# An attention kernel's last reciprocals, branch, closing products, first keys and order of work

## The chip, the cores and the metric

The kernel runs on one core of one Trainium2 chip. A core has five engines that run side by side, each with a list of instructions in a fixed order: PE (matmuls; its weight loads are shown apart as PEld), DVE (VectorE), ACT (ScalarE), POOL (GpSimd) and SP (SyncE), which here issues DMAs. Engines wait for one another through semaphores. The metric is the time of one execution on the device, in microseconds (us); lower is better. A profile gives the start and length of each instruction of one execution.

## The reference

Two attention layers read two inputs of 2048 x 512; their outputs stand side by side. Cut to what matters:

```python
# A: 32 query heads of 16, one shared key and value head
q = (x @ wq).reshape(B, S, 32, 16);  k = x @ wk;  v = x @ wv
p = softmax(einsum("bhqd,bkd->bhqk", q, k) * 16**-0.5)
a = einsum("bhqk,bkd->bhqd", p, v).reshape(B, S, 512) @ wo
# B: linear attention, 32 heads of 16
phi(t) = concat(softmax(t @ w_phi), softmax(-(t @ w_phi)))
o = phi(q) @ (phi(k).T @ v) / (phi(q) @ phi(k).sum(0) + 1e-6)
b = o.reshape(B, S, 512) @ wo
out = concat(a, b)
```

A's exponentials are nearly all of the work: 32 heads x 2048 queries x 2048 keys.

## The kernel before, in words

**Tiles of A.** Scores are made keys down, queries across. A unit is 128 keys x 512 queries of one head: one matmul with 32 rows of contraction (L1672). Four heads make a quad and use the four row groups of PE. A stage `sc` of 0 to 31 is eight heads' even or odd half for 512 queries: 16 quads, one per 128 keys (`kap`). Most quads go to ACT, which takes the exponential of three units (1536 columns) and of two units (1024 columns) by turns, out of PSUM banks 0 to 2 and 3 to 4 (L1733; jobs `qk` for the scores and `ex` for the exponential). While ACT reads one group of banks, PE may fill the other only. The other quads (`dq`) are done on DVE: it turns scores into the bits of an exponential with a multiply and an add (L1834, `dz`), adds shifts to make three further terms (two on DVE, L1852, `dS`; one on POOL, L1849, `dP`), and PE sums the four terms (L1889, `dpv`). The products with the values (L1778, `pv`; L1889) gather in one PSUM bank, `ACC`. The values carry a block of ones, so that 16 rows of each 32 in `ACC` are sums of exponentials, the denominators, and 16 are numerators; even and odd stages have them the other way round.

**End of a stage.** DVE copies `ACC` to SBUF (`ac`, L1449). SP's DMAs gather the denominators (L1905), DVE takes reciprocals (`rc`, L1913), four DMAs put them back as one row per group of 32 (L1918), and four more spread each row over 16 partitions (L1924). POOL, in the last stages DVE, multiplies (`on`, L1931). For odd stages DMAs then move the rows (L1937). PE multiplies by `wo` (L1950; for the last 512 queries, in parts, `pp`, L1970).

**The last stage (31)** goes another way, in `finish_last`, in two halves of 256 queries. DVE copies the denominators over each group of 32 partitions out of `ACC` (stream shuffle, L1980), ACT takes a logarithm (L1982) and an exponential of its negative (L1983), which is the reciprocal, DVE multiplies (L1996), and PE adds the last part of the output product (L2004) to parts made before (L1970). ACT and DVE copy the four results out (L2014, L1449), and four DMAs of 128 KB write them (L2016).

**Start.** POOL fills a tile with ones and one with zeros; PE multiplies them ten times (`WARM`, L1443). Then it makes the first queries and the first 512 keys by turns (L1604), 512 columns each. ACT copies the queries (L1610), DVE the keys with the even half masked out and with the odd half masked out (L1616). A first score group needs the queries and the masked keys.

**Other work** between: all of B, spread over the run by release times; zero products (L1443 and L1426) where the plan leaves PE idle.

**What sets the order.** `_Fast.run` places jobs one by one on a modelled time line with fixed durations, by earliest start and rank; `SEEDS` holds a number for each 20 us of modelled time, which shakes the ranks and picks among a few settings. The result is one fixed list per engine. The chip runs each list in that order, and only semaphores set the times.

**The branch.** Whether the inputs stay in the bounds that this fast path needs is computed as a flag. Each engine reads it and branches; DVE and SP do so before their last pieces (`cut`), so that their last instructions stand behind a jump. In `plan`, DVE's cut is set from its last nine jobs.

## Time and profile before

| | us |
|---|---|
| median of 3 runs (740.68 to 740.93) | 740.73 |
| the profiled execution | 740.4 |
| its span | 738.7 |
| ACT busy | 719.0 (97%) |
| PE busy | 696.7 (94%) |
| DVE busy | 676.7 (92%) |
| POOL busy | 316.8 (43%) |
| granted PE clock, mean | 0.994 of full speed |

The span runs from the profile's first to its last record; the execution's time has 1.7 us more around it. "Busy" counts an instruction from its start to its end; instructions of ACT and of PE overlap their neighbours a little, so a mean duration is longer than the pitch from one start to the next. In a timeline row stand start, length, engine, line, operation, output<-input, sizes, a count where several are merged, and in brackets the idle time before it and what ended it.

### The profile page before, as it was taken

To read this page: it belongs to the slowest core of one execution; us is meant where nothing else is said; L and a number is where in the kernel's file an instruction comes from. 1 tells how busy PE (TensorE), PEld (TensorE's weight loads), DVE (VectorE), ACT (ScalarE), POOL (GpSimd) and SP (SyncE) were. 2 spreads that over 40 slices of the span, in tenths; PEclk is the share of its full clock that TensorE was granted. 3 is DMA by queue.
4 is the path that set the end of the run, shared out by engine and by line. 5 is a ranking of instruction groups with operands and counts; after the bars stand their busy time and mean duration, and the time that the engine had idled before them with its cause. 6 is when DMAs were issued, how large, how long until landed. Compare 5 with 4: busy or idle time off the path is not lost.

```text
span 738.7 us, 17787 instructions
## 1 busy us (share of the span) xinstructions
PE 696.7 (94%) x7467; PEld 227.5 (31%) x7467; DVE 676.7 (92%) x1134; ACT 719.0 (97%) x675; POOL 316.8 (43%) x248
## 2 busy tenths in 40 slices
PE   8999999999999999999999999999999999999995
PEld 3233233323332222223332322233333333333331
DVE  4999999999999999997999999899999999999992
ACT  6999999999999999999999999999999999999993
POOL 6335453542535435447343534444443443334441
PEclk9999999999999999999999999999999999999997
DMA  9820011110111101111011111011111111112102
GB/s 191 190 32 6 8 8 10 12 9 6 10 12 17 30 7 8 13 9 9 7 8 19 23 23 12 3 19 17 30 20 8 15 22 27 23 18 25 16 20 40
DMA packets 47552, 18.13 MB, mean 25 GB/s; under 512 B 38500, under 2 KB 45604, under 8 KB 47464
## 3 DMA queue, kind: packets, MB, share of 16 engines
q1 hardware_dynamic: 45736, 16.62, 17.2%
q8 instruction: 60, 0.98, 0.5%
q10 hardware_dynamic: 1728, 0.30, 0.2%
q14 instruction: 28, 0.23, 0.1%
HBM read 2.15 MB, written 4.19 MB: 9 GB/s over the span
## 4 chain that ended last, share of the span: by engine, by line
ACT 85%; PE 9%; DVE 3%; DMA 1%; POOL 1%; SPq 1%; issue 0%; POOLq 0%; DVEq 0%
ACT f_PT L1733 81%; PE f_ps L1672 3%; ACT f_Ek L2121 2%; ACT f_ET L2214 2%; PE f_ps L1889 1%; DVE f_Z L1834 1%; PE f_ps L1778 1%; PE f_ps L1443 1%; DVE f_Z L1852 1%; PE f_ps L2300 1%; POOL f_Z L1849 1%; PE f_ps L1662 1%; DMA f_denS<-f_denS 0%; PE f_ps L1970 0%; DMA f_denS<-f_denC 0%
## 5 line engine op out<-in xcount | busy, mean ns | idle before, releaser
L1733 ACT ACTIVATE f_PT<-f_ps 128x1536 bf16<-128x1536 f32 (+1 forms) x603 | 691.7, 1369 | 1.3 <-PE f_ps L1672 1.0
L1849 POOL TENSOR_TENSOR f_Z<-f_Z,f_step 128x1024 int32<-128x1024 int32 x135 | 255.3, 1891 | 352.8 <-DVE f_Z L1852 351.0
L1834 DVE TENSOR_SCALAR f_Z<-f_ps 128x512 int16<-128x512 f32 x540 | 351.5, 681 | 21.1 <-PE f_ps L1672 14.2
L1672 PE MATMUL f_ps<-f_QA,f_KR 32*128 32x512 bf16 x2048 | 303.9, 384 | 29.8 <-ACT f_PT L1733 16.8
L1852 DVE TENSOR_SCALAR f_Z<-f_Z 128x2048 int16<-128x2048 int16 x270 | 182.5, 694 | 1.5 <-PE f_ps L1889 0.4
L1672 PEld LDWEIGHTS f_ps<-f_QA,f_KR 32*128 32x128 bf16 x2048 | 78.9, 91 | 264.1 <-ACT f_PT L1733 167.5
L1889 PE MATMUL f_ps<-f_Z,f_VK 128*32 128x512 f16 x2160 | 141.1, 382 | 0.2
L1778 PE MATMUL f_ps<-f_PT,f_VA 128*32 128x512 bf16 x1508 | 124.3, 385 | 0.0
L1443 PE MATMUL f_ps<-f_ones,f_zero 128*128 128x512 bf16 (+8 forms) x281 | 65.8, 355 | 1.3 <-POOL f_zero L1469 1.3
L1889 PEld LDWEIGHTS f_ps<-f_Z,f_VK 128*32 128x32 bf16 x2160 | 45.5, 96 | 63.3 <-issue 26.4
L1778 PEld LDWEIGHTS f_ps<-f_PT,f_VA 128*32 128x32 bf16 x1508 | 26.7, 94 | 57.2 <-issue 55.3
L1443 PEld LDWEIGHTS f_ps<-f_ones,f_zero 128*128 128x128 bf16 (+2 forms) x281 | 18.7, 97 | 29.7 <-issue 23.7
L1426 PE MATMUL f_ps<-f_ones,f_zero 32*128 32x512 bf16 x74 | 26.1, 380 | 0.0
L1931 POOL TENSOR_TENSOR f_Od<-f_accS,f_denS 128x512 bf16<-128x512 f32 x14 | 17.8, 1269 | 16.1 <-DVE f_Z L1852 15.2
L2270 DVE TENSOR_TENSOR f_Wk<-f_ps,f_wq 128x512 bf16<-128x512 f32 x32 | 21.9, 683 | 0.6 <-PE f_ps L2260 0.4
L1449 DVE COPY f_accS<-f_ps 128x512 f32<-128x512 f32 x31 | 21.2, 683 | 1.4 <-PE f_ps L1778 0.9
L1931 POOL TENSOR_TENSOR f_On<-f_accS,f_denS 128x512 bf16<-128x512 f32 x14 | 17.8, 1271 | 9.8 <-DVE f_Z L1852 8.1
L2152 DVE TENSOR_TENSOR f_vS<-f_ps,f_rs 128x1024 bf16<-128x1024 f32 x16 | 19.4, 1217 | 1.5 <-PE f_ps L2142 1.5
L2127 DVE TENSOR_REDUCE f_ssum<-f_Ek 128x64 f32<-128x1024 bf16 x16 | 19.3, 1209 | 1.6 <-ACT f_Ek L2121 1.3
L2214 ACT ACTIVATE f_ET<-f_ps 128x512 bf16<-128x512 f32 x32 | 19.6, 744 | 0.0
L2121 ACT ACTIVATE f_Ek<-f_ps 128x512 bf16<-128x512 f32 x32 | 19.6, 756 | 0.0
L2300 PE MATMUL f_ps<-f_Bwo,f_oT 128*128 128x512 bf16 x64 | 16.6, 381 | 0.3 <-ACT f_ET L2214 0.3
(104 smaller groups left out, 339.4 us busy)
## 6 DMA issues: line engine op xcount, KB each, us to landing
f_denS<-f_denS SPq DMA_DIRECT2D x124, 30.0 KB, 3.1
out_dram<-f_outB SPq DMA_DIRECT2D x17, 128.0 KB, 2.0
f_denC<-f_accS SPq DMA_DIRECT2D x124, 2.0 KB, 1.7
f_denS<-f_denC SPq DMA_DIRECT2D x124, 2.0 KB, 1.7
out_dram<-f_outA SPq DMA_DIRECT2D x14, 128.0 KB, 2.2
f_On<-f_Od SPq DMA_DIRECT2D x60, 16.0 KB, 1.8
f_Bwv<-in_B_wqkv_dram SPq DMA_DIRECT2D x1, 512.0 KB, 4.3
f_Bwo<-in_B_wo_dram SPq DMA_DIRECT2D x1, 512.0 KB, 5.3
```

Source lines behind the costliest of these rows:

```text
L1426: self.add("pe", lambda pe: pe.matmul(out, lhsT=zero[0:32, :], rhs=rhs, start=False, stop=False, tile_position=(0, 0)), reads=["ones", "ze ...
L1443: mm = pe.matmul(ps[x:x + m, bank, 0:n].rearrange("p (a n) -> p a n", n=128), lhsT=zero[0:r, 0:m], rhs=rhs, start=start, stop=start, **kw)
L1672: return pe.matmul(self.ps[:, bank, :], lhsT=self.KR[32 * g:32 * g + 32, sc % 2, kap * 128:(kap + 1) * 128], rhs=self.QA[32 * g:32 * g + 3 ...
L1733: self.add("act", lambda a: a.activation(out=PT[:, sl[0]:sl[0] + size, :], in_=ps[:, b0:b0 + size, :], func=ACT.Exp), reads=[("PS", b0 + i ...
L1778: mm = pe.matmul(ps[32 * g:32 * g + 32, bank, :], lhsT=w, rhs=PT[:, slots[g], :], start=start, stop=stop, tile_position=(0, 32 * g))
L1834: self.add("dve", lambda v: v.tensor_scalar(out=o, in0=ps[:, bank, :], scalar1=self.Z1, scalar2=self.Z0, op0=ALU.mult, op1=ALU.add), reads ...
L1849: self.add("pool", lambda g: g.tensor_tensor(out=w(t), in0=w(0), in1=self.step3.to_broadcast([128, 256 * (b - a)]), op=ALU.add), reads=zk ...
L1852: self.add(eng, lambda v: v.tensor_scalar(out=Z[:, t, a:b], in0=Z[:, 0, a:b], scalar1=256.0 * t, scalar2=None, op0=ALU.add), reads=zk, wri ...
L1889: mm = pe.matmul(ps[32 * g:32 * g + 32, bank, :], lhsT=w[:, k, :], rhs=Zf[:, k, sl[g], :], start=start and k == 0, stop=stop and k == 3, t ...
L1931: self.add("pool" if sc < self.ONP else "dve", lambda v: v.tensor_tensor(out=o, in0=accS[:, r, :], in1=R[:, r, :], op=ALU.mult), reads=[(" ...
L2121: self.add("act", (lambda a, sg: (lambda e: e.activation(out=Ek[:, r, a].rearrange("p h f -> p (h f)"), in_=ps[:, bank, :], func=ACT.Exp, ...
L2214: self.add("act", lambda e: e.activation(out=self.ET[:, sl, :], in_=self.ps[:, bank, :], func=ACT.Exp, scale=sg), reads=[("PS", bank)], wr ...
```

## The change

Six edits:

1. For stage 30, the last with reciprocals by DMA, the four spreading DMAs are left out. A DVE stream shuffle over 128 x 512 (job `sh`) spreads the row; the multiplication `on` 30 waits for it.
2. DVE's cut: the last nine DVE jobs are sorted by planned start, the planned end of PE is appended, and the largest gap is always taken (before: only gaps over 0.5 us that begin over 5 us ahead of PE's end).
3. In the closing chain zero products may be put ahead of the last products where the plan has over two of them to spare, and the planned readiness of the two halves is a little later.
4. At the start PE makes the queries and the first 128 keys only, by turns; the whole first 512 keys follow as a projection of their own. DVE masks the 128 keys first (even half), then the other 384. The first score groups wait for the 128 alone.
5. Nine zero products at the start in place of ten; planned arrivals of the first input tile at 5.6 and 6.35 us (4.8 and 6.0 before).
6. New `SEEDS`, hence another order throughout. Each kind of work keeps its count, but for zero products and the pieces named above.

```diff
-    WARM = 10
+    WARM = 9
...
-            self.tw["AxT", 0, c] = ((4.8, 6.0, 6.0, 6.0)[c], "sp")
+            self.tw["AxT", 0, c] = ((5.6, 6.35, 6.35, 6.35)[c], "sp")
...
-                job(("pk", 0), "pe", 0.44, self.proj_first, mode="full", nb=2, prio=0)
+                job(("pf",), "pe", 0.54, self.proj_first, mode="full", nb=1, prio=0)
+                job(("qa", 0), "act", 0.478, self.proj_first2, after=[("pf",)], frees=[("pq", 0)], prio=0)
+                job(("KR0",), "dve", 0.25, lambda: self.proj_k3(0, 0, 128), after=[("pf",)], prio=0)
+                job(("pk", 0), "pe", 0.87, lambda: self.proj_k(0), after=[("pf",)], mode="full", nb=1, prio=0)
+                job(("KR", 0, 0), "dve", 0.52, lambda: self.proj_k3(0, 128, 512), after=[("pk", 0), ("KR0",)], prio=u)
...
+        job("sh", "dve", 0.85, self.spread, after=[("rc", 30)], prio=1.3)
...
-                after=[("rc", sc)] + ([("op", 4 * ((sc - 12) // 8) + i) for i in range(4)] if sc >= 12 else []))
+                after=[("rc", sc) if sc < 30 else "sh"] + ([("op", 4 * ((sc - 12) // 8) + i) for i in range(4)] if sc >= 12 else []))
...
-            for w, name, rd in ((self.wq[:, :, 0:128], ("pq", 0), ("wq", 0)), (self.wk_rep, ("pk", 0), "wk_rep")):
+            for w, name, rd, n in ((self.wq[:, :, 0:128], ("pq", 0), ("wq", 0), 512), (self.wk_rep, None, "wk_rep", 128)):
...
+    def kr(self, u):
+        return ("KR0",) if u[0] % 2 == 0 and u[1] == 0 else ("KR", u[0] % 2, u[1] // 4)
...
         self.dmas(fs, [("denR", r)], [("row", r), ("denS", r)], 1.8)
+        if sc == 30:
+            return
...
+    def spread(self):
+        R = self.denS[:, 0, :]
+        self.add("dve", lambda v: v.stream_shuffle(out=R, in_=R, mask=[0] * 16 + list(range(16, 32))), reads=[("row", 0), ("denS", 0)], writes=[("row", 0), ("denS", 0)])
...
-        ready = [t + 2.1, t + 2.8]
+        ready = [t + 2.15, t + 2.95]
...
+            k = int((ready[n] - t) / 0.2155) - 1
+            if k > 0:
+                self.fill(cols=(512,) * k, start=True, bank=next(b for b in self.free if b not in (6, 7)))
...
-    SEEDS = (841236, 504472, 983516, 719862, 658977, 503735, 772408, 265022, 493407, 762606, 12760, 907041, 734584,
+    SEEDS = (332850, 31012, 1022942, 986432, 402629, 324809, 0, 27406, 912665, 397942, 417505, 51469, 741216,
...
-        ends = [x for x in self.log if x[2] == "dve"][-9:]
-        gaps = [(b[0] - a[0] - a[1], n) for n, (a, b) in enumerate(zip(ends, ends[1:])) if a[0] + a[1] < self.te["pe"] - 5.0]
-        self.cut["dve"] -= 8 - max(gaps)[1] if gaps and max(gaps)[0] > 0.5 else 0
+        ends = sorted((x for x in self.log if x[2] == "dve"), key=lambda x: x[0])[-9:] + [(self.te["pe"], 0.0)]
+        gaps = [(b[0] - a[0] - a[1], n) for n, (a, b) in enumerate(zip(ends, ends[1:]))]
+        self.cut["dve"] -= 8 - max(gaps)[1]
```

With the change the lines from L1555 on move: L1672 becomes L1681, L1778 L1790, L1834 L1846, L1849 L1861, L1852 L1864, L1889 L1901, L1662 L1671, L1913 L1925, L1918 L1930, L1931 L1949, L1970 L1988, L1980 L1998, L1996 L2014, L2004 L2025.

PE at the start, from the last of its four pairs of products for queries and keys to the second score group (L1604 and L1608 the pairs, L1594 a projection of 512 keys, L1443 zero products, L1641 the values). Before:

```order
L1604 MATMUL f_ps<-f_AxT,f_wq 128x512
L1604 MATMUL f_ps<-f_AxT,f_wk_rep 128x512
L1672 MATMUL f_ps<-f_QA,f_KR 128x512 x3
L1443 MATMUL f_ps<-f_ones,f_zero 128x512 x4
L1672 MATMUL f_ps<-f_QA,f_KR 128x512 x2
```

With the change:

```order
L1608 MATMUL f_ps<-f_AxT,f_wq 128x512
L1608 MATMUL f_ps<-f_AxT,f_wk_rep 128x128
L1594 MATMUL f_ps<-f_AxT,f_wk_rep 128x512 x4
L1681 MATMUL f_ps<-f_QA,f_KR 128x512 x3
L1641 MATMUL f_ps<-f_wv,f_AxT 128x16 x16
L1681 MATMUL f_ps<-f_QA,f_KR 128x512 x2
```

The key half of each pair has shrunk from 512 to 128 columns, and the whole 512 keys now stand between the pairs and the first scores, where before nothing stood.

PE in the middle, around the sixth of the query projections that are made on the way (L1662 before, L1671 now). Before:

```order
L1778 MATMUL f_ps<-f_PT,f_VA 32x512 x4
L2170 MATMUL f_ps<-f_vS,f_Ek 32x34 x32
L1778 MATMUL f_ps<-f_PT,f_VA 32x512 x4
L1672 MATMUL f_ps<-f_QA,f_KR 128x512 x3
L1778 MATMUL f_ps<-f_PT,f_VA 32x512 x4
L1662 MATMUL f_ps<-f_AxT,f_wq 128x512 x4
L1672 MATMUL f_ps<-f_QA,f_KR 128x512 x6
```

With the change:

```order
L1901 MATMUL f_ps<-f_Z,f_VK 32x512 x16
L1790 MATMUL f_ps<-f_PT,f_VA 32x512 x8
L1681 MATMUL f_ps<-f_QA,f_KR 128x512 x4
L1901 MATMUL f_ps<-f_Z,f_VK 32x512 x16
L1790 MATMUL f_ps<-f_PT,f_VA 32x512 x4
L1671 MATMUL f_ps<-f_AxT,f_wq 128x512 x4
L1681 MATMUL f_ps<-f_QA,f_KR 128x512 x3
```

Between two neighbouring score groups for ACT there now stand 16 sums of DVE's terms, four products with the values and the projection; the row of four scores is a group of two for ACT and two for DVE.

DVE at the end, from the last reciprocals to the end of its list. Before:

```order
L1913 RECIPROCAL f_denC<-f_denC 128x16
L1834 TENSOR_SCALAR f_Z<-f_ps 128x512 x2
L1852 TENSOR_SCALAR f_Z<-f_Z 128x2048 x2
L1834 TENSOR_SCALAR f_Z<-f_ps 128x512 x3
L1852 TENSOR_SCALAR f_Z<-f_Z 128x2048
L2490 BRANCH_PREFETCH_HINT
L1852 TENSOR_SCALAR f_Z<-f_Z 128x2048
L1931 TENSOR_TENSOR f_On<-f_accS,f_denS 128x512
L2494 TENSOR_LOAD flag
L2497 COMPARE_AND_BRANCH
L1980 STREAM_SHUFFLE f_ET<-f_ps 128x256 x2
```

With the change:

```order
L1925 RECIPROCAL f_denC<-f_denC 128x16
L1846 TENSOR_SCALAR f_Z<-f_ps 128x512 x4
L1864 TENSOR_SCALAR f_Z<-f_Z 128x2048 x2
L1846 TENSOR_SCALAR f_Z<-f_ps 128x512 x3
L1943 STREAM_SHUFFLE f_denS<-f_denS 128x512
L1864 TENSOR_SCALAR f_Z<-f_Z 128x2048
L2511 BRANCH_PREFETCH_HINT
L1864 TENSOR_SCALAR f_Z<-f_Z 128x2048
L1949 TENSOR_TENSOR f_On<-f_accS,f_denS 128x512
L2515 TENSOR_LOAD flag
L2518 COMPARE_AND_BRANCH
L1998 STREAM_SHUFFLE f_ET<-f_ps 128x256 x2
```

The last reciprocals stand two score conversions earlier. The new shuffle stands ahead of the last two shifts. The flag and the branch stand where they stood: behind the last `on`, ahead of the closing shuffles.

PE at the end, from the last score group. Before:

```order
L1672 MATMUL f_ps<-f_QA,f_KR 128x512 x3
L1970 MATMUL f_ps<-f_wo,f_On 128x512
L1889 MATMUL f_ps<-f_Z,f_VK 32x512 x16
L1778 MATMUL f_ps<-f_PT,f_VA 32x512 x4
L1970 MATMUL f_ps<-f_wo,f_On 128x512
L1778 MATMUL f_ps<-f_PT,f_VA 32x512 x4
L1970 MATMUL f_ps<-f_wo,f_On 128x512 x9
L2004 MATMUL f_ps<-f_wo,f_Od 128x512 x2
L1970 MATMUL f_ps<-f_wo,f_On 128x512 x4
L2004 MATMUL f_ps<-f_wo,f_Od 128x512 x2
```

With the change:

```order
L1681 MATMUL f_ps<-f_QA,f_KR 128x512 x3
L1988 MATMUL f_ps<-f_wo,f_On 128x512 x2
L1790 MATMUL f_ps<-f_PT,f_VA 32x512 x4
L1988 MATMUL f_ps<-f_wo,f_On 128x512 x2
L1901 MATMUL f_ps<-f_Z,f_VK 32x512 x16
L1790 MATMUL f_ps<-f_PT,f_VA 32x512 x4
L1988 MATMUL f_ps<-f_wo,f_On 128x512 x10
L2025 MATMUL f_ps<-f_wo,f_Od 128x512 x2
L1988 MATMUL f_ps<-f_wo,f_On 128x512
L2025 MATMUL f_ps<-f_wo,f_Od 128x512 x2
```

Four output parts, not two, stand ahead of the last products with the values, and the last sum of DVE's terms (16 matmuls) has moved behind three of these groups. One part stands between the two closing pairs, not four. No zero product (L1443) stands in this list's end: with this order the condition of edit 3 is not met.

More of the change, by code (lines that the diff above doesn't have):

```diff
@@ L1560, in jobs_a @@
             if ch == 0:
[L1561 to L1562 removed]
+                job(("aq", 0), self.AENG, self.ADUR, lambda: self.absmax(self.QA[:, 0, :], 4, [("QA", 0)]), after=[("qa", 0)], prio=6, rel=14.0)
                 continue
@@ L1590, in fn @@
             return mm
-        self.add("pe", fn, reads=[("AxT", kc), "wk_rep"], writes=[("PS", bank)])
+        self.add("pe", fn, reads=self.ax(kc) + ["wk_rep"], writes=[("PS", bank)])
     def proj_first(self):
@@ L1596, in proj_first, with fn, proj_k3 @@
         if self.rec is None:
-            a, b = self.bk["pk", 0]
-            self.bk["pk", 0], self.bk["pq", 0] = [a], [b]
+            self.bk["pq", 0] = self.bk["pf",]
         for dc in range(4):
-            for w, name, rd in ((self.wq[:, :, 0:128], ("pq", 0), ("wq", 0)), (self.wk_rep, ("pk", 0), "wk_rep")):
-                bank = self.bank(name)
-                def fn(pe, dc=dc, w=w, bank=bank):
-                    return pe.matmul(ps[:, bank, :], lhsT=w[:, dc, :], rhs=xT[:, dc, 0:512], start=(dc == 0), stop=(dc == 3))
+            for w, name, rd, n in ((self.wq[:, :, 0:128], ("pq", 0), ("wq", 0), 512), (self.wk_rep, None, "wk_rep", 128)):
+                bank = self.bank(name) if name else self.ACC
+                def fn(pe, dc=dc, w=w, bank=bank, n=n):
+                    return pe.matmul(ps[:, bank, 0:n], lhsT=w[:, dc, :], rhs=xT[:, dc, 0:n], start=(dc == 0), stop=(dc == 3))
                 kw = dict(accum=[("PS", bank)]) if dc else dict(writes=[("PS", bank)])
                 self.add("pe", fn, reads=[("AxT", 0, dc // 2), rd], **kw)
+    def proj_k3(self, e, a, b):
+        ps, bank, half = self.ps, self.bank(("pk", 0)) if a else self.ACC, self.half
+        self.add("dve", lambda v: v.tensor_scalar(out=self.KR[:, e, a:b], in0=ps[:, bank, a:b], scalar1=half[:, e:e + 1], scalar2=None, op0=ALU.mult),
+                 reads=[("PS", bank), "half1"] + [("half", g) for g in range(4)], writes=[("KR", e, 0) if a else ("KR0",)])
     def proj_first2(self):
```

15 lines of the change are left out of this document (7 added, 8 removed).

## The prediction

> **What bounds the kernel now.** I read the page first, then the busy time by stretches, the chain of waits, and the timelines of both ends. From the page, the chain's shares by engine and the costliest group:
>
> ```profile
> ACT 85%; PE 9%; DVE 3%; DMA 1%; POOL 1%; SPq 1%; issue 0%; POOLq 0%; DVEq 0%
> L1733 ACT ACTIVATE f_PT<-f_ps 128x1536 bf16<-128x1536 f32 (+1 forms) x603 | 691.7, 1369 | 1.3 <-PE f_ps L1672 1.0
> ```
>
> ACT's exponentials are the bound. Whether they can get denser is told by two rows of the chain, where groups stand back to back, and by the stretches from the first exponential (9.12) to the end of the last (723.75) and behind it (columns: stretch, length, then busy time of PE, PEld, DVE, ACT, POOL, the granted clock, DMA share, GB/s):
>
> ```profile
> 67.39 0.98 ACT f_Ek L2121 x2
> 577.52 83.69 ACT f_PT L1733 x74
> ...
> 9.12:723.75 714.63, 683.47 (x7425) 223.30 (x7423) 671.20 (x1123) 714.33 (x667) 310.19 (x221) 1.00 0.17 22
> 728.83:734.37 5.54, 3.59 (x8) 1.04 (x8) 2.54 (x6) 2.52 (x6) 0.00 (x0) 0.58 0.16 49
> ...
> 733.00:734.00 1.00, 1.00 (x4) 0.15 (x2) 0.00 (x0) 0.00 (x0) 0.00 (x0) 0.50 0.78 243
> ```
>
> A group takes 83.69/74 = 1.131 us, 603 take 682.0; B's 64 small exponentials, two in 0.98, take 31.4. That is 713.4 of 714.63: the middle wastes 1.2 us in all. ACT's list keeps its counts under the change, so a new order can win at most 1.2 there. What can be won otherwise lies ahead of 9.12 and behind 723.75, which I call E; the profile ends at 738.70, E+14.95.
>
> **The start.** Its timeline:
>
> ```profile
> 1.33 4.45 PE L1443 MATMUL f_ps<-f_ones,f_zero 128*128 128x512 bf16 x10 [1.33 <-POOL f_zero L1469]
> 5.64 0.10 PEld L1604 LDWEIGHTS f_ps<-f_AxT,f_wq 128*128 128x128 bf16 x1 [0.77 <-DMA f_wq<-in_A_wq_dram]
> 5.67 0.57 PE L1604 MATMUL f_ps<-f_AxT,f_wq 128*128 128x512 bf16 x1
> 6.05 0.40 PE L1604 MATMUL f_ps<-f_AxT,f_wk_rep 128*128 128x512 bf16 x1
> 7.37 0.38 PE L1604 MATMUL f_ps<-f_AxT,f_wk_rep 128*128 128x512 bf16 x1
> 7.57 0.60 ACT L1610 ACTIVATE f_QA<-f_ps 128x512 bf16<-128x512 f32 x1 [5.47 <-PE f_ps L1604]
> 7.78 1.41 DVE L1616 TENSOR_SCALAR f_KR<-f_ps,f_half 128x512 bf16<-128x512 f32 x2 [6.58 <-PE f_ps L1604]
> 8.68 0.39 PE L1672 MATMUL f_ps<-f_QA,f_KR 32*128 32x512 bf16 x3 [0.94 <-DVE f_KR L1616]
> 9.12 5.99 ACT L1733 ACTIVATE f_PT<-f_ps 128x1536 bf16<-128x1536 f32 x5 [0.96 <-PE f_ps L1672]
> 11.12 1.04 PE L1589 MATMUL f_ps<-f_AxT,f_wk_rep 128*128 128x512 bf16 x4
> ...
> 697.49 0.40 PE L2260 MATMUL f_ps<-f_KVn,f_ET 128*128 128x128 bf16 x4
> ```
>
> The first pair waits for a DMA (5.64), not for the zero products, so the tenth, taken away, gains nothing. From 6.05 to 7.37 products follow every 0.22. A key product of 128 columns costs between a quarter of that and all of it; four of them take 0.40 with their tail in the last row, so I take 0.06. Then: first pair 0.38 + 0.10 (the clock is still rising), three pairs of 0.28, to 6.99; the new projection of 512 keys, four by 0.22 and 0.08 for the change of kind (1.04 whole in its row), to 7.95; scores there, and the exponential 0.44 later (8.68 to 9.12), at 8.4. What runs beside it is ready by then: ACT's queries at 7.7 (last query product ends 0.38 after 6.71, then 0.60), DVE's 128 keys by 7.6 (under half of a 512's 0.7). **Gain 0.7**; with key products at full price it would be 0.1.
>
> **The middle.** The order can win 1.2 or lose; the place shown with the change tells how. From one score group to the next but one stand 16 + 8, 4, 16 + 4 + 4 and 3 matmuls. By pitch (16 column-tiled are four passes of 0.22) that is 0.88 + 0.44 + 0.4 + 0.88 + 0.22 + 0.88 + 0.4, with 0.1 at each of six changes of kind 4.7. ACT meanwhile has three groups and one pair of B's, 3 x 1.131 + 0.98 = 4.4. Here it waits some 0.3. Such places are few in both lists. I take **a loss of 0.4**, bounds a gain of 1.2 and a loss of 3.
>
> **The end.** Two views; first the chain of waits from the last reciprocals on:
>
> ```profile
> 714.00 0.16 DVE f_denC L1913
> ...
> 714.76 0.59 SPq L1918
> ...
> 716.03 2.93 DMA f_denS<-f_denC
> ...
> 721.69 3.46 DMA f_denS<-f_denS
> ...
> 725.18 0.70 DVE f_On L1931
> ...
> 725.93 1.70 PE f_ps L1970 x7
> 727.63 1.17 issue
> ...
> 728.83 0.45 DVE f_ET L1980
> ...
> 730.20 0.49 DVE f_Od L1996
> ...
> 730.74 1.03 PE f_ps L2004 x2
> 731.78 1.71 PE f_ps L1970 x4
> 733.48 0.87 PE f_ps L2004 x2
> ...
> 734.37 0.69 DVE f_outA L1449
> ```
>
> and the timeline:
>
> ```profile
> 717.67 0.65 PE L1672 MATMUL f_ps<-f_QA,f_KR 32*128 32x512 bf16 x3
> 718.10 0.69 DVE L1834 TENSOR_SCALAR f_Z<-f_ps 128x512 int16<-128x512 f32 x1 [0.38 <-PE f_ps L1672]
> 718.82 1.29 DVE L1852 TENSOR_SCALAR f_Z<-f_Z 128x2048 int16<-128x2048 int16 x2
> 720.20 1.89 POOL L1849 TENSOR_TENSOR f_Z<-f_Z,f_step 128x1024 int32<-128x1024 int32 x1 [1.70 <-DVE f_Z L1852]
> 721.77 0.39 PE L1672 MATMUL f_ps<-f_QA,f_KR 32*128 32x512 bf16 x3
> 722.41 1.05 PE L1889 MATMUL f_ps<-f_Z,f_VK 128*32 128x512 f16 x16
> 723.93 0.40 PE L1778 MATMUL f_ps<-f_PT,f_VA 128*32 128x512 bf16 x4
> 728.80 0.01 DVE L1980 LOAD_MASK_SELECT f_ET<-f_ps  x1 [2.93 <-issue]
> 730.96 0.48 DVE L1996 SCALAR_TENSOR_TENSOR f_Od<-f_ps,f_odd,f_ET 128x256 bf16<-128x256 f32 x1 [0.27 <-ACT f_ET L1983]
> ```
>
> `ACC` is complete at 724.33, E+0.58, but DVE sits in its list behind `on` 30, which waits for the spreading DMAs till 725.18, and then spends 2.93 on flag and branch. Only at E+5.08 do the closing shuffles start.
>
> *DVE with the change.* Its last score conversion ends at 718.79, E-5.0, held by PE's scores (717.67), and those by ACT, so I leave it. The new shuffle of 512 columns costs between one 256-column shuffle of this trace and two (0.45 to 0.90); I take 0.85, since it grows with columns. Then the two shifts, 1.3, to E-2.85, and `on` at once, 0.7, to E-2.1; branch to E+0.8. The shuffle waits for nothing if the rows have landed: that took 4.96 from the reciprocals (714.00 to 718.96), and nine DVE operations of at least 0.56 to 0.6 stand between now, 5.2 or more. On SP the four moves of `on` 29 now stand right ahead of these DMAs: four issues of 0.59, 2.4, and DVE has four operations between, also 2.4, so SP is free just in time. The four spreading issues that go were followed on SP by the last writes alone. Behind the shuffle is queued the last shift, for which POOL (1.89) and PE wait: POOL would end at E-0.9.
>
> *PE with the change.* From the last scores (E-1.98) to the 16 sums it took 0.64 with one part between; now three parts more (0.66) and the products with the values between two changes of kind (0.42): sums at E-0.26, later than POOL's end. They take 0.88, the last products 0.40: `ACC` complete at E+1.0, 0.4 later than before. That, not the branch, is now last: **shuffles at E+1.1, 4.0 earlier**. The spreading DMAs and the branch are no longer on the path; DVE's cover for the branch is 0.2 to 0.3 us.
>
> *The chain behind it.* The first closing pair is ready 1.91 after the shuffle (728.83 to 730.74), the second 2.65 (730.96 + 0.48 + the same 0.05): E+3.0 and E+3.75. PE meanwhile makes ten parts from E+1.1, 0.22 each, to E+3.3. Before, PE stood idle from 727.63 to 730.74, the granted clock fell to 0.58 over the stretch and to 0.50, and eight closing products took 3.61. With no idle time they go at 0.22: pair to E+3.75, one part to E+3.95, pair to E+4.4, its end E+4.55, against 734.35, E+10.6. From there to the end it took 4.35 (last copy, DMA, what follows). The four writes of 128 KB now start within 1 us instead of in two pairs 2.5 apart; one takes 0.54 at the 243 GB/s of 733 to 734, so the last may wait 0 to 1.1; I take 0.4. The end lies at E+9.3, **a gain of 5.6**. Zero products in the closing chain cost and give nothing: the list has none.
>
> **Sum.** -0.7 + 0.4 - 5.6 = -5.9, the span 732.8, the profiled execution 734.5 of 740.4. The median of the runs shown lies 0.33 above it: **734.8**.
>
> **Rivals.** *Cold start* (0.12). With nine zero products PE idles from about 5.2 to 5.64, in just the stretch that ended with the clock rising (0.38 for the pair at 5.67, 0.22 from 6.05 on). If it then does not rise, products cost 0.43 (4.45/10): pairs 2.15, projection 1.7, scores at 9.6, exponential at 10.15. That is 1.0 worse than before, not 0.7 better: 736.5. Against it: from 1.33 to 6.05 PE is still nine tenths busy. The Trainium skill, "TensorE: Matmul & The Clock Gate", Part 1, says the clock is released after a busy window of about 3.4 us, free-running; by that rule a broken window may push release one window on, and no run here yet shows what share of it suffices.
>
> *The branch is not covered* (0.08), and the edit of the cut moves nothing, which the lists bear out: flag and jump stand where they stood. The prefetch hint stands one shift ahead of `on`, which no longer waits 5.06 for a DMA. If the 2.93 was short only because the hint was 9.3 early (719.5 to 728.80), shuffles come at up to E+5.8: the end's first 4.0 is lost and 0.7 more, 739.5. For: a wait labelled "issue" names no cause. Against: even with that lead it cost 2.93.
>
> *Slower* (0.05): score groups late in PE's list, as at the place in the middle, often enough. At 0.4 a place the gain is gone after 15 places, and 18 give 742. A wait of 12 ns on average per group would do the same. For: the order is new everywhere. Against: ACT's idle time before its exponentials was 1.3 in all, in a list as full.
>
> **How the numbers follow.** Forecast 0.75, its own range 733.4 to 736.2; cold start 0.12; branch 0.08; slower 0.05. Range 733.0 to 737.6. A change of 0.2%, 1.5 us, is about what can be told from none; below 739.25 lie the forecast, the cold start and a third of the branch: faster 0.90, same 0.05, slower 0.05.
>
> **What would show it.** First exponential near 8.4 with products every 0.22; E near 723.4; `on` 30 right behind the last shift, no spreading DMA; closing shuffles within 0.2 of `ACC`'s last product, not of the branch; closing pairs at full clock; 9.3 from E to the end. Wrong if the shuffle waits long for a DMA, the idle time ahead of L1998 stays "issue", or ACT's idle time passes 4 us.

## The result, and the profile after

The changed kernel takes 734.86 us (median of 4 runs, 734.5 to 735.21) against 740.7 (4 runs): a ratio of 0.9926, with a 95% interval of 0.9909 to 0.9943. The profiled execution took 734.78, its span is 733.0. The page's shares of the chain and the costliest group:

```profile
ACT 88%; PE 7%; DVE 3%; DMA 1%; SPq 0%; issue 0%
L1745 ACT ACTIVATE f_PT<-f_ps 128x1536 bf16<-128x1536 f32 (+1 forms) x603 | 693.0, 1373 | 1.3 <-PE f_ps L1681 0.7
```

ACT's 603 groups are as before, and DVE, DMA and "issue" have not grown. Where the time came from is read by stretches. From the first exponential to the end of the last (now 723.81, again called E), the closing chain, and what lies behind it (columns as in the prediction):

```profile
8.66:723.81 715.15, 683.94 (x7447) 224.48 (x7449) 670.89 (x1127) 714.48 (x667) 310.69 (x225) 1.00 0.17 23
724.88:728.16 3.28, 3.28 (x15) 1.19 (x13) 2.46 (x7) 2.27 (x6) 0.00 (x0) 1.00 0.01 2
728.16:733.00 4.84, 0.01 (x1) 0.00 (x0) 0.74 (x2) 0.48 (x1) 0.00 (x0) 0.91 0.35 113
```

The first exponential comes 0.46 earlier (8.66, before 9.12), the middle is 0.52 longer (715.15, before 714.63): together nothing. ACT's idle time inside the middle, its length less ACT's busy time, has grown from 0.30 (714.63 less 714.33) to 0.67 (715.15 less 714.48). The 1.3 of the page's row hides that, because it contains the wait ahead of the first exponential, 0.96 before and 0.66 now. From E to the end it takes 9.19 instead of 14.95. **The end is the whole gain, 5.76.** In the closing chain PE is busy for 3.28 of 3.28 at a granted clock of 1.00; before, it was 3.59 of 5.54 at 0.58.

The start, in the timeline:

```profile
1.32 3.95 PE L1443 MATMUL f_ps<-f_ones,f_zero 128*128 128x512 bf16 x9 [1.32 <-POOL f_zero L1469]
5.70 0.38 PE L1608 MATMUL f_ps<-f_AxT,f_wq 128*128 128x512 bf16 x1 [0.42 <-DMA f_AxT<-in_A_x_dram]
5.96 0.38 PE L1608 MATMUL f_ps<-f_AxT,f_wq 128*128 128x512 bf16 x1
6.71 0.39 PE L1608 MATMUL f_ps<-f_AxT,f_wq 128*128 128x512 bf16 x1 [0.31 <-DMA f_AxT<-in_A_x_dram]
7.26 1.03 PE L1594 MATMUL f_ps<-f_AxT,f_wk_rep 128*128 128x512 bf16 x4
```

The clock is up from the first product on, though PE had idled for 0.42. Then the second half of the first input is late: the third pair waits 0.31 for it. Shorter key products brought PE to that landing early.

The end, in the timeline:

```profile
718.43 0.72 DVE L1943 STREAM_SHUFFLE f_denS<-f_denS 128x512 f32<-128x512 f32 x1
719.06 1.28 DVE L1864 TENSOR_SCALAR f_Z<-f_Z 128x2048 int16<-128x2048 int16 x2
720.25 0.68 DVE L1949 TENSOR_TENSOR f_On<-f_accS,f_denS 128x512 bf16<-128x512 f32 x1
721.01 1.89 POOL L1861 TENSOR_TENSOR f_Z<-f_Z,f_step 128x1024 int32<-128x1024 int32 x1 [2.56 <-DVE f_On L1949]
723.56 1.05 PE L1901 MATMUL f_ps<-f_Z,f_VK 128*32 128x512 f16 x16
724.43 0.39 PE L1790 MATMUL f_ps<-f_PT,f_VA 128*32 128x512 bf16 x4
724.75 2.33 PE L1988 MATMUL f_ps<-f_wo,f_On 128*128 128x512 bf16 x10
724.88 0.01 DVE L1998 LOAD_MASK_SELECT f_ET<-f_ps  x1 [3.95 <-PE f_ps L1790]
726.92 0.59 PE L2025 MATMUL f_ps<-f_wo,f_Od 128*128 128x512 bf16 x2
727.57 0.59 PE L2025 MATMUL f_ps<-f_wo,f_Od 128*128 128x512 bf16 x2
```

`on` 30 stands behind the last shift and waits for no DMA. DVE is then idle for 3.95, and the closing shuffles are let go by `ACC`'s last product, at E+1.07. Where the branch runs is told by the records of the flag's load and of the jump, which the view of their source lines has (`DVEq` is DVE's sequencer; least, middle and longest duration in ns, then the start). Before:

```profile
L2494 DVEq TENSOR_LOAD <-flag x1: 541/541/541, 725.2 to 725.2; - x1
L2497 DVEq COMPARE_BRANCH  x1: 84/84/84, 725.8 to 725.8; - x1
```

With the change:

```profile
L2515 DVEq TENSOR_LOAD <-flag x1: 544/544/544, 719.2 to 719.2; - x1
L2518 DVEq COMPARE_BRANCH  x1: 84/84/84, 719.8 to 719.8; - x1
```

Before, the load began with `on` (725.18), when the DMA that `on` waits for had landed, and the first instruction behind the jump came 3.6 after it, at 728.80. With the change it began at 719.2, when the new shuffle was over (719.15), 1.05 ahead of `on`. If it takes the same 3.6, an estimate, the branch is through at 722.8, some 2 ahead of `ACC`. Ten parts fill PE until the first closing pair at E+3.11; the last product ends at 728.16, E+4.35. No zero product stands in the closing chain: that edit does nothing in this order. The rule for the cut does nothing here either: flag and branch stand behind `on` 30, as before.

### The profile page after: what moved, and what is told of

Same layout as the page of the kernel before. It is cut to its first block, busy times and chain, and to the rows that moved or that the text cites. A ratio compares the mean times of both kernels' runs of the same rounds, so it can differ in the third digit from the quotient of the medians.

```text
span 733.0 us, 17847 instructions
## 1 busy us (share of the span) xinstructions
PE 694.9 (95%) x7498; PEld 228.4 (31%) x7498; DVE 675.0 (92%) x1137; ACT 719.1 (98%) x675; POOL 316.6 (43%) x248
## 4 chain that ended last, share of the span: by engine, by line
ACT 88%; PE 7%; DVE 3%; DMA 1%; SPq 0%; issue 0%
ACT f_PT L1745 84%; PE f_ps L1681 2%; ACT f_Ek L2142 2%; ACT f_ET L2235 2%; PE f_ps L1901 1%; DVE f_Z L1846 1%; PE f_ps L1790 1%; DMA f_AxT<-in_A_x_dram 1%; DVE f_Z L1864 1%; PE f_ps L1988 0%; PE f_ps L1968 0%; PE f_ps L2321 0%; PE f_ps L1443 0%; DVE f_outA L1449 0%; SPq L1460 0%; DVE f_outB L1449 0%
## 5 line engine op out<-in xcount | busy, mean ns | idle before, releaser
L1861 POOL TENSOR_TENSOR f_Z<-f_Z,f_step 128x1024 int32<-128x1024 int32 x135 | 255.4, 1892 | 349.6 <-DVE f_Z L1864 342.9
L1846 DVE TENSOR_SCALAR f_Z<-f_ps 128x512 int16<-128x512 f32 x540 | 351.7, 683 | 23.8 <-PE f_ps L1681 21.4
L1681 PE MATMUL f_ps<-f_QA,f_KR 32*128 32x512 bf16 x2048 | 303.3, 384 | 28.0 <-ACT f_PT L1745 19.0
L1864 DVE TENSOR_SCALAR f_Z<-f_Z 128x2048 int16<-128x2048 int16 x270 | 180.8, 693 | 0.8
L1681 PEld LDWEIGHTS f_ps<-f_QA,f_KR 32*128 32x128 bf16 x2048 | 79.5, 91 | 261.9 <-ACT f_PT L1745 166.4
L1901 PE MATMUL f_ps<-f_Z,f_VK 128*32 128x512 f16 x2160 | 141.3, 382 | 0.2
L1790 PE MATMUL f_ps<-f_PT,f_VA 128*32 128x512 bf16 x1508 | 121.7, 385 | 0.5 <-DVE f_accS L1449 0.4
L1443 PE MATMUL f_ps<-f_ones,f_zero 128*128 128x512 bf16 (+10 forms) x303 | 72.7, 344 | 1.3 <-POOL f_zero L1469 1.3
L1901 PEld LDWEIGHTS f_ps<-f_Z,f_VK 128*32 128x32 bf16 x2160 | 45.7, 96 | 62.3 <-issue 25.4
L1790 PEld LDWEIGHTS f_ps<-f_PT,f_VA 128*32 128x32 bf16 x1508 | 25.7, 94 | 54.6 <-issue 51.3
L1443 PEld LDWEIGHTS f_ps<-f_ones,f_zero 128*128 128x128 bf16 (+2 forms) x303 | 20.6, 97 | 31.6 <-issue 25.8
L1949 POOL TENSOR_TENSOR f_Od<-f_accS,f_denS 128x512 bf16<-128x512 f32 x14 | 17.8, 1270 | 16.6 <-DVE f_Z L1864 15.7
L1949 POOL TENSOR_TENSOR f_On<-f_accS,f_denS 128x512 bf16<-128x512 f32 x14 | 17.8, 1270 | 15.6 <-DVE f_Z L1864 14.6
```

The source lines that it names most:

```text
L1443: mm = pe.matmul(ps[x:x + m, bank, 0:n].rearrange("p (a n) -> p a n", n=128), lhsT=zero[0:r, 0:m], rhs=rhs, start=start, stop=start, **kw)
L1681: return pe.matmul(self.ps[:, bank, :], lhsT=self.KR[32 * g:32 * g + 32, sc % 2, kap * 128:(kap + 1) * 128], rhs=self.QA[32 * g:32 * g + 3 ...
L1790: mm = pe.matmul(ps[32 * g:32 * g + 32, bank, :], lhsT=w, rhs=PT[:, slots[g], :], start=start, stop=stop, tile_position=(0, 32 * g))
L1846: self.add("dve", lambda v: v.tensor_scalar(out=o, in0=ps[:, bank, :], scalar1=self.Z1, scalar2=self.Z0, op0=ALU.mult, op1=ALU.add), reads ...
L1861: self.add("pool", lambda g: g.tensor_tensor(out=w(t), in0=w(0), in1=self.step3.to_broadcast([128, 256 * (b - a)]), op=ALU.add), reads=zk ...
L1864: self.add(eng, lambda v: v.tensor_scalar(out=Z[:, t, a:b], in0=Z[:, 0, a:b], scalar1=256.0 * t, scalar2=None, op0=ALU.add), reads=zk, wri ...
```

## The experiments

**Theory 1**: the closing shuffles start when the latest of three is done (`ACC`'s last product, `on` 30, flag with branch); to take the branch off that wait is enough. **Theory 2**: the spreading DMAs' time is the gain. **Theory 3**: the start or the order carries a part. The kernels were each run in the same batch as the kernel before; ratios are against that batch (before had medians of 740.76, 740.3 and 740.24 in them). In the profiles, "shuffles" is the row of their first instruction:

| kernel | median, us | ratio (95%) | first exponential | middle | shuffles | end of span |
|---|---|---|---|---|---|---|
| before | 740.7 | | 9.12 | 714.63 | E+5.05 | E+14.95 |
| changed | 734.86 | 0.9926 (0.9909 to 0.9943) | 8.66 | 715.15 | E+1.07 | E+9.19 |
| changed, again | 734.83 | 0.9918 (0.9901 to 0.9934) | 8.37 | 715.16 | E+1.08 | E+9.57 |
| before + shuffle alone | 735.15 | 0.9924 (0.9908 to 0.9941) | 9.64 | 714.65 | E+0.82 | E+9.01 |
| before + branch's place alone | 736.08 | 0.9948 (0.9929 to 0.9967) | 9.12 | 715.90 | E+2.12 | E+10.48 |
| before + 13 zero products | 738.98 | 0.9988 (0.9978 to 0.9997) | 8.86 | 714.63 | E+4.81 | E+13.01 |
| changed, spread by DMA | 734.71 | 0.9924 (0.9907 to 0.9941) | 8.26 | 715.16 | E+0.65 | E+9.18 |
| the same, branch behind `on` | 736.81 | 0.9943 (0.9927 to 0.9960) | 8.52 | 715.14 | E+2.90 | E+11.54 |
| changed, branch out of the way | 734.94 | 0.9932 (0.9912 to 0.9951) | 8.78 | 715.16 | E+1.08 | E+9.26 |
| changed, no table | 743.55 | 1.0053 (1.0033 to 1.0073) | 8.76 | 724.48 | E+1.50 | E+9.96 |
| changed, 5 zero products | 736.26 (one run) | | 9.97 | 715.16 | E+1.08 | E+9.37 |
| changed, 10 zero products | 734.9 (one run) | | 8.58 | 715.14 | E+1.08 | E+9.38 |
| changed, full key products | 735.45 (one run) | | 9.23 | 715.15 | E+1.08 | E+9.32 |

**The changed kernel once more**, unedited, to see how much of each number is chance.

> The changed kernel once more, as the measure for the others of this call: 734.9, between 734.4 and 735.4. E (end of ACT's last score exponential) near 723.8, closing shuffles near E+1.1, end of the span near E+9.2.

The middle repeats to 0.01, the shuffles to 0.01. The first exponential does not (8.37, 8.66), since the first input's landing scatters, nor does the end of the span: the last copies are over at E+5.09 both times, and the 0.38 by which E+9.57 is later lie in the last write and what follows it.

**Shuffle undone, two ways.** The spreading goes by DMA again. In the first kernel the rule for the branch then puts it ahead of `on` 30; in the second it stays behind, so that this kernel has neither of the edits to DVE's list, only the new start and order. In both the planner also sets PE's last products in another order than in the changed kernel: two output parts, not four, stand ahead of the last products with the values, and `ACC` is complete at E+0.6.

```diff
-        job("sh", "dve", 0.85, self.spread, after=[("rc", 30)], prio=1.3)
+        job("sh", "dve", 0.0, self.spread, after=[("rc", 30)], prio=1.3)
-        if sc == 30:
+        if False:
-        self.add("dve", lambda v: v.stream_shuffle(...))
+        return
 # second kernel only:
-        self.cut["dve"] -= 8 - max(gaps)[1]
+        pass
```

> Edit 1 undone in the changed kernel: stage 30's rows are spread by DMA again, with no shuffle; the order up to the last score group is kept, and by the rule of edit 2 the branch falls ahead of `on` 30, into the wait for the DMA. Theory 1 (the closing shuffles start when the latest of three things is done: ACC's last product, `on` 30, the flag and branch; taking the branch off the wait is enough): from the reciprocals to the spread rows it took 11.0 before (714.16 to 725.16); now from 712.8 to 723.8, `on` to 724.5, shuffles at 724.6, no later than in the changed kernel: 734.9, within 0.6. Theory 2 (the gain is the spreading DMAs' time, and the shuffle is what saves it): `on` 30 ends 4 later than in the changed kernel (724.5 against 720.9) and the end follows: 738 to 739.

> As the run before, but the branch kept behind `on` 30, as in the kernel before. Theory 1: `on` ends at 724.5, flag and branch add 2.9, shuffles at 727.4 instead of 724.9, PE idles over 2 ahead of its first closing pair: 737.4 if the clock holds, up to 739 if it falls and the closing products double. The difference to the run before is then the branch's own price, 2.5 to 4. Theory 2: no difference between the two, both 738 to 739.

The timeline of the first:

```profile
722.60 0.69 DVE L1949 TENSOR_TENSOR f_On<-f_accS,f_denS 128x512 bf16<-128x512 f32 x1 [3.15 <-DMA f_denS<-f_denS]
724.07 0.01 DVE L1998 LOAD_MASK_SELECT f_ET<-f_ps  x1 [0.78 <-PE f_ps L1790]
```

and of the second:

```profile
712.39 0.24 DVE L1925 RECIPROCAL f_denC<-f_denC 128x16 f32<-128x16 f32 x1
722.78 0.69 DVE L1949 TENSOR_TENSOR f_On<-f_accS,f_denS 128x512 bf16<-128x512 f32 x1 [3.09 <-DMA f_denS<-f_denS]
726.56 0.01 DVE L1998 LOAD_MASK_SELECT f_ET<-f_ps  x1 [3.09 <-PE f_ps L1988]
728.50 0.60 PE L2025 MATMUL f_ps<-f_wo,f_Od 128*128 128x512 bf16 x2 [2.00 <-DVE f_Od L2014]
728.95 1.24 PE L1988 MATMUL f_ps<-f_wo,f_On 128*128 128x512 bf16 x3
```

The second's closing chain by stretch:

```profile
726.56:731.05 4.49, 2.53 (x7) 0.72 (x7) 2.50 (x7) 2.50 (x6) 0.00 (x0) 0.79 0.13 40
```

In both, `on` waits some 3.1 us for the spreading DMAs. In the first the branch is run inside that wait, the shuffles follow `ACC`, and nothing is lost. In the second it follows `on`: 3.09 pass, 2.1 us of the time are gone. The row names PE's parts as the releaser, but these write no tile that the shuffle reads; the label is the last event before it, and what stands there in DVE's list is the flag's load and the jump. PE idles 2.00, and the clock falls during the three parts behind the pair. Theory 2 is wrong (it asked for 738 to 739 in the first kernel, measured 734.71); theory 1 holds, with the branch at 2.1 instead of the 2.5 to 4 expected, and the time at 736.81 instead of 737.4 or more.

The second kernel also bears on theory 3. It lacks the shuffle, and its branch stands where it stood before, yet it takes 3.95 less than the kernel before. The new order has the last reciprocals 1.4 earlier against E (712.39, E-11.3; before 713.92, E-9.8), `on` is over at E-0.2 instead of E+2.1, and the closing shuffles start at E+2.90 instead of E+5.05.

**The shuffle alone**, in the kernel before, its order, start and rule for the branch kept:

```diff
+        job("sh", "dve", 0.85, self.spread, after=[("rc", 30)], prio=1.3)
-                after=[("rc", sc)] + (...))
+                after=[("rc", sc) if sc < 30 else "sh"] + (...))
+        if sc == 30:
+            return
+    def spread(self): ...
```

> Edit 1 alone, in the kernel before: the new shuffle for stage 30 behind the last two shifts, no spreading DMAs; PE's list, the start and the branch's place as before. Theory 1: shifts end at 720.1, shuffle 0.7, `on` 0.7, branch 2.9: shuffles of the closing chain at 724.5, E+0.7; nine parts, pairs at full clock, last product at 728.3: 734.9 within 0.5, all that the whole change brought. Theory 3 (start and order carry part of the gain): 0.5 to 1.5 above the changed kernel.

```profile
721.37 1.81 DVE L1938 TENSOR_TENSOR f_On<-f_accS,f_denS 128x512 bf16<-128x512 f32 x1
725.11 0.01 DVE L1987 LOAD_MASK_SELECT f_ET<-f_ps  x1 [1.93 <-PE f_ps L1779]
...
724.90 0.21 issue
...
L2504 DVEq COMPARE_BRANCH  x1: 84/84/84, 722.0 to 722.0; - x1
```

This timeline has the whole gain: `on` ends at 723.18, E-1.1, and the end of span is at E+9.01. The branch is nearly covered, not quite. The line of 724.90, from the chain of waits, shows `ACC`'s last product over at 724.90 and 0.21 of "issue" up to the shuffles, where the changed kernel's shuffles follow that product within 0.06. The last line is the jump's own record: it ran at 722.0, beside `on`, and the first instruction behind it came 3.1 later, as in the kernel before (725.85 to 728.80, 2.95). So the 1.93 is again the branch under PE's name.

The start and the order, which this kernel lacks, add nothing that can be told to what the shuffle brings. Theory 3 falls in that sense alone: without the shuffle, the kernel above shows, start and order bring 3.95.

**The branch's place alone**, in the kernel before, the spreading DMAs kept:

```diff
-        ends = [x for x in self.log if x[2] == "dve"][-9:]
-        gaps = [... for n, (a, b) in enumerate(zip(ends, ends[1:])) if a[0] + a[1] < self.te["pe"] - 5.0]
-        self.cut["dve"] -= 8 - max(gaps)[1] if gaps and max(gaps)[0] > 0.5 else 0
+        ends = sorted((x for x in self.log if x[2] == "dve"), key=lambda x: x[0])[-9:] + [(self.te["pe"], 0.0)]
+        gaps = [... for n, (a, b) in enumerate(zip(ends, ends[1:]))]
+        self.cut["dve"] -= 8 - max(gaps)[1]
```

> The kernel before with the change's rule for the place of VectorE's flag and branch alone (they fall ahead of `on` 30; the spreading by DMA, the ten zero products and the order of the work stay). Theory 1 (the closing shuffles start when the latest of `ACC`'s last product, `on` 30 and flag with branch is done; what the next cause costs is what remains): the branch is run while VectorE waits for the spreading DMAs; `on` 30 ends where it did, about E+2.2, and the shuffles start there instead of E+5.08: 2.9 earlier. PE then has almost no idle time, its clock stays up, and some 1.3 of the 5.6 comes with that: end at E+10.7, 736.5 us. Theory 2 (the spreading DMAs' wait is what counts, the branch little): end at E+14 or later, 740. Theory 3 (a wait of the same length moves elsewhere): `on` 30 lands later by as much, shuffles at E+5, 740.7.

```profile
726.52 0.69 DVE L1931 TENSOR_TENSOR f_On<-f_accS,f_denS 128x512 bf16<-128x512 f32 x1 [5.13 <-DMA f_denS<-f_denS]
727.14 0.01 DVE L1980 LOAD_MASK_SELECT f_ET<-f_ps  x1
729.49 1.03 PE L1970 MATMUL f_ps<-f_wo,f_On 128*128 128x512 bf16 x4
```

The shuffles follow `on` with no gap at E+2.12, the closing products run at full clock, the end is at E+10.48: 4.47 of the 5.76 with the DMAs still in the way. Now the DMAs are what is last, and they cost the remaining 1.3. (The profiled execution took 737.25, the three others 736.0 to 736.2; its middle is 1.3 longer by a fall of the clock that the last section shows.)

**The clock alone**: 13 zero products where PE stood idle ahead of the first closing pair, in the kernel before.

```diff
+            if n == 0:
+                self.fill(cols=(512,) * 13, start=True, bank=next(b for b in self.free if b not in (6, 7)))
             t = max(t, ready[n])
```

> The kernel before with 13 zero products of 512 columns on PE between its ninth closing part and the first closing pair, where it stood idle from 727.63 to 730.74; nothing else moves. Theory 1 (part of the gain is the clock: the eight closing products took 3.61 because PE had idled, and the first pair's own time is set by VectorE): the first pair still starts at E+7.0, the clock stays up, the pair, the four parts and the second pair take 0.43 + 0.87 + 0.43 and the last one's tail, end of the last product at E+8.9 instead of E+10.6: 1.7 earlier, 739.0 us. Rival (the closing products are slow for another reason, their operands or the banks that ScalarE and VectorE read beside them): they still take 3.6, 740.7. Rival (the zero products are in the way, because they start late or run at half speed): first pair later than E+7.2, 741 or more.

The timeline:

```profile
727.13 2.97 PE L1443 MATMUL f_ps<-f_ones,f_zero 128*128 128x512 bf16 x13
728.30 0.01 DVE L1980 LOAD_MASK_SELECT f_ET<-f_ps  x1 [2.75 <-PE f_ps L1970]
730.25 0.60 PE L2006 MATMUL f_ps<-f_wo,f_Od 128*128 128x512 bf16 x2
```

and the closing chain by stretch:

```profile
728.33:732.15 3.82, 3.67 (x17) 1.28 (x14) 2.50 (x6) 2.27 (x6) 0.00 (x0) 1.00 0.01 2
```

The branch is still there (2.75, again under PE's name). The clock stays at 1.00, and the first pair to the last product takes 1.90 (730.25 to 732.15) instead of 3.61. In this profile that is worth 1.7 of the 1.94 by which the end is nearer to E. The runs give less: a ratio of 0.9988, 0.2 to 1.6 us. What an idle PE costs differs from run to run of the kernel before (738.65 to 740.98 in 13), perhaps by where the fall of the clock lands, which is not shown; the profile of before took 740.4, one of the dear ones.

**The branch out of the way altogether**, in the changed kernel:

```diff
-        self.cut = {e: len(p) for e, p in self.S.prog.items() if e in ("dve", "sp")}
+        self.cut = {e: len(p) for e, p in self.S.prog.items() if e == "sp"}
```

> The changed kernel with VectorE's flag and branch moved out of the way altogether: the engine's jump comes behind its share of the closing chain, so no branch stands ahead of the closing shuffles. Theory 1 (the branch is covered by the wait for `ACC`'s last product, which lasted 0.8 to 4 us on the shuffles): no difference, shuffles at E+1.1, 734.8 within 0.4. Rival (fetching the block behind the jump still costs the closing chain something, by a queue or instruction fetch): up to 0.5 faster here, 734.3. Rival (a branch must be paid somewhere, and behind the chain it delays the last copies): slower by up to 2.9 us, 737.

There is no difference, in time (734.94) or in the shuffles (E+1.08): the branch is fully covered in the changed kernel.

**No table**: all seeds at zero.

```diff
-    SEEDS = (332850, 31012, ...)
+    SEEDS = (0,) * 37
```

> The changed kernel with every seed of the order's table at zero: the planner's rules are the same, only the tie-breaking that the table sets differs, in all parts. Theory 1 (the middle is bound by ACT's exponentials, and the order is worth what the idle time ahead of them is): the order's worth is read off the stretch from the first to the last score exponential, 715.15 with the change's table, 714.64 with the table of before; without a table 716 to 719, the time 736 to 739, nearly all of the difference inside that stretch. Rival (the order's worth lies in the closing chain, which the table's last entries set): the stretch stays within 0.5 and what follows E lengthens by 1 to 3 us, 736 to 738. Rival (the table is worth nothing): 734.8 within 0.5.

```profile
L1745 ACT ACTIVATE f_PT<-f_ps 128x1536 bf16<-128x1536 f32 x608 | 698.1, 1344 | 4.0 <-PE f_ps L1681 2.9
660.00:670.00 10.00, 8.69 (x85) 2.40 (x83) 8.69 (x16) 7.75 (x8) 5.50 (x3) 0.83 0.29 39
```

The loss is in the middle, as theory 1 has it, but more than twice the most that was expected: 9.3. ACT has 608 groups instead of 603, 5 x 1.131 = 5.7, and 4.0 idle instead of 1.3, which is 8.4 of it. Of the idle time 2.25 stands between 660 and 670 alone (second line), where the clock fell; this execution took 744.94, 1.4 above the median. So the order itself is worth about 7 in the middle, most of it the five groups. The table thus decides not only when, but how many quads go to ACT; the expectation missed that. The tables of before and of the change agree in that count, which the prediction's bounds for the middle took for granted.

**The start**, in three kernels: five zero products, ten, and full key products.

```diff
-    WARM = 9
+    WARM = 5      # second kernel: 10
 # third kernel:
-... (self.wk_rep, None, "wk_rep", 128)):
+... (self.wk_rep, None, "wk_rep", 512)):
```

> The changed kernel with 5 zero products at the start instead of 9 (nothing else differs): PE is busy from about 1.3 to 3.5 only and then idle for 2 us until the first input lands. Theory 1 (the clock rises on work done in a window before, so the zero products decide it): the first products go at 0.4 instead of 0.22, the new projection ends later, the first exponential at about 9.8 to 10.2 instead of 8.3 to 8.7, the time 736.3. Rival (the clock rises with the projection's own products soon enough, or a time after the first work regardless of the gap): the first exponential at 8.3 to 8.8, 734.8.

> The changed kernel with ten zero products at the start, as before, instead of nine. Theory 1 (the start is set by the first input's landing, not by the zero products; the clock rises within the first products either way): first exponential at 8.2 to 8.8, 734.8. Rival (the tenth is what brings the clock up in time in the changed kernel): all products at 0.22 from the first on, first exponential at 8.2 or earlier. Rival (the tenth is in the way): the first pair 0.1 to 0.4 later than the landing, first exponential near 9.

> The changed kernel with the key products of its first four pairs at 512 columns instead of 128; the new projection of all 512 keys stays behind them, so the extra columns are work done twice. It tells apart what sets the first exponential. If PE's products do (0.16 more for each of four pairs): 0.5 to 0.65 later, 9.2. If the landing of the input's second half does (a wait of 0.31 stood between the second and the third pair): only the last two pairs count fully, 0.3 to 0.35 later, 8.9 to 9.0. The time 735.2.

The timeline with five:

```profile
1.33 2.31 PE L1443 MATMUL f_ps<-f_ones,f_zero 128*128 128x512 bf16 x5 [1.33 <-POOL f_zero L1469]
5.62 0.59 PE L1608 MATMUL f_ps<-f_AxT,f_wq 128*128 128x512 bf16 x1 [1.97 <-DMA f_AxT<-in_A_x_dram]
7.70 1.90 PE L1594 MATMUL f_ps<-f_AxT,f_wk_rep 128*128 128x512 bf16 x4
9.97 3.71 ACT L1745 ACTIVATE f_PT<-f_ps 128x1536 bf16<-128x1536 f32 x3 [1.53 <-PE f_ps L1681]
```

Here is the prediction's cold start: PE idles 1.97, the projection takes 1.90 instead of 1.03, the first exponential comes at 9.97, and the time is 736.26. The rival's price was nearly right (10.15 and 736.5 were worked out), its condition was not met with nine. With ten:

```profile
5.65 0.38 PE L1608 MATMUL f_ps<-f_AxT,f_wq 128*128 128x512 bf16 x1 [0.48 <-DMA f_AxT<-in_A_x_dram]
6.63 0.39 PE L1608 MATMUL f_ps<-f_AxT,f_wq 128*128 128x512 bf16 x1 [0.28 <-DMA f_AxT<-in_A_x_dram]
```

the same picture as with nine, the wait for the input's second half too. With full key products:

```profile
5.74 0.58 PE L1608 MATMUL f_ps<-f_AxT,f_wq 128*128 128x512 bf16 x1 [0.40 <-DMA f_AxT<-in_A_x_dram]
6.53 0.38 PE L1608 MATMUL f_ps<-f_AxT,f_wq 128*128 128x512 bf16 x1
9.23 3.71 ACT L1745 ACTIVATE f_PT<-f_ps 128x1536 bf16<-128x1536 f32 x3 [0.82 <-PE f_ps L1681]
```

the first exponential is 0.57 later than in the changed kernel, as if PE's products alone set it. But the clock rose only at about 6.5 in this execution, so that PE came to the third pair after the landing; the two causes are not cleanly apart. And the unedited start scatters from 8.26 to 8.78, so one run does not tell what the short key products are worth.

## Why the prediction was right, step by step

The forecast was 734.8, measured 734.86. Its terms one by one:

**The start, -0.7**: -0.46 in the profile. The step that took four pairs back to back from the first input's landing left out that this input comes in halves; the row at 6.71 has a wait of 0.31 for the second. Over the seven profiles of the changed start with nine or ten zero products (8.26 to 8.78, mean 8.56) and the four with the start of before (8.86 to 9.64, mean 9.19) it is 0.6.

**The middle, +0.4**: +0.52, and the same to 0.02 in every kernel with the changed table whose middle ran undisturbed. Of it, 0.37 is idle time of ACT inside the middle (0.67, before 0.30), so waits at single places did grow, as the step supposed; they are too short to be labelled one by one, and which instructions cause them was not settled. The step's size was a guess between its bounds, and that it came so near is luck.

**The end, -5.6**: -5.76. Its steps: the new shuffle 0.72 (0.85 taken); `on` over at 720.93, E-2.9 (E-2.1): DVE stood 0.3 earlier, the shuffle took 0.13 less, and rows on DVE overlap their neighbours by 0.1 each; 16 sums at E-0.25 (E-0.26); shuffles at E+1.07 (E+1.1), and let go by `ACC`, as stated; first pair at E+3.11 (E+3.3), last product over at E+4.35 (E+4.55); then 4.84 (4.75, with 0.4 taken for the writes; 5.2 in the repetition). POOL's last shift ended at E-0.91 (E-0.9), and that is luck: its tile was ready 0.6 earlier than forecast (720.34, E-3.47), but it started only at 721.01, behind `on`, which the last section takes up. The split of the gain that the prediction gave, shuffles 4.0 earlier and the rest from the clock, is borne out by three profiles: the branch's place alone 4.47 with the clock, the clock alone 1.94, the shuffle alone 5.94. In the runs the clock's share is smaller (0.2 to 1.6).

**What the prediction did not see** is that three edits shorten the same wait. The shuffle alone brings 5.6 us of the median, the rule for the branch's place alone 4.2, the new order (with the start) without either 3.95. The changed kernel, where the rule moves nothing, has 5.8 to 5.9: the parts do not add up, because what each of them leaves to be gained is only the time down to `ACC`. Its rival "the branch is not covered" asked whether 2.93 would still fit; the cover is not the 0.2 to 0.3 it named but some 2, since the load of the flag began with the end of the new shuffle, ahead of `on`, and not behind it as the step had it (branch to E+0.8; by the records to about E-1). The kernel with the branch out of the way shows that nothing is left of it. The step was wrong there without effect on the sum, because `ACC` is later in either case. That the hint's lead sets the price, as the rival feared, did not show: in the kernel with the shuffle alone the jump came 2.6 behind the hint (719.38 to 721.96), before 6.9 (718.84 to 725.77), and from the jump on they took 3.1 and 3.0.

**Cold start** (0.12) and **slower** (0.05) did not come. The run with five zero products shows that the first was a real mechanism. The run without a table shows that an order can lose as much as the second asked for, though most of that comes from five more groups on ACT and not from late score groups.

## What to carry to other kernels

A jump costs what is not covered by a wait that the engine has anyway: look for the longest wait ahead of the last instructions and put the flag's load and the branch inside it. An edit that brings nothing on top of another can still bring much without it, so run each alone before calling it idle. Ahead of a short closing chain, count PE's idle time twice, once as it is and once for the clock that falls with it. Read a releaser's name against what the waiting instruction reads: the 3.09, 2.75 and 1.93 above bear PE's name and are a branch. The load of the flag and the jump have records of their own, which say when they ran.

## What the runs showed that was not expected

**DVE and POOL exclude one another in some operations.** In the timelines, DVE's product of two SBUF tiles takes 0.68, but 1.81 in the kernel with the shuffle alone (its row at 721.37, above), beside this:

```profile
720.74 1.89 POOL L1850 TENSOR_TENSOR f_Z<-f_Z,f_step 128x1024 int32<-128x1024 int32 x1 [1.69 <-DVE f_Z L1853]
```

and 1.48 at one place of the changed kernel:

```profile
705.68 3.86 POOL L1861 TENSOR_TENSOR f_Z<-f_Z,f_step 128x1024 int32<-128x1024 int32 x2 [3.65 <-DVE f_Z L1864]
708.61 1.48 DVE L1949 TENSOR_TENSOR f_Od<-f_accS,f_denS 128x512 bf16<-128x512 f32 x1
```

Both end 0.55 after POOL's operation (722.63 and 723.18; 709.54 and 710.09), as if they could only begin behind it. The other way round, in the end of the changed kernel POOL's last shift starts 0.08 after `on` is over, though its tile was ready at 720.34. The Trainium skill, "Trainium Architecture — The Big Picture", "What this means for kernel authors", says that these two engines share a port pair under an exclusive lock; these rows agree. It cost nothing in the changed kernel, as `ACC` was later.

**The granted clock can fall with hardly any idle time ahead of it.** In the profile of the branch's place alone, by stretch:

```profile
340.00:350.00 10.00, 9.52 (x102) 3.37 (x102) 6.03 (x10) 10.00 (x14) 7.05 (x6) 1.00 0.22 14
350.00:352.50 2.50, 2.50 (x24) 0.67 (x27) 1.33 (x4) 1.32 (x3) 0.22 (x1) 0.50 0.05 13
352.00:354.00 2.00, 2.00 (x17) 0.46 (x15) 1.94 (x4) 1.53 (x2) 0.00 (x0) 0.65 0.10 25
```

PE had been busy for 9.52 of 10, the clock fell to 0.50 from 350.0 to about 353.4, some 3.4 us, and ACT waited 1.18; the middle of that execution is 715.90, against 714.63 to 714.65 in the three other profiles with this list, which have no such fall. In the kernel without a table the clock fell for as long (0.83 over the 10 us of 660 to 670), there behind 1.11 in which PE had been idle. The Trainium skill, "TensorE: Matmul & The Clock Gate", Part 1, ties the fall to an idle window in its table of the two states; by the busy time that the profile shows, the first rows do not fit that. Such falls may be one reason why single runs differ by over 1 us; parts of a microsecond are better read from stretches of a profile than from medians. On the rise, the free-running window of that part of the Trainium skill fits: with nine zero products it came between the first product (5.70) and about 6.8, in executions of the same start.
